# A PSUM bank chosen by its last reader, one more batch transposed by DMA, and key beacons first in the load queue

## The chip, the cores and the metric

The kernel runs on one core of one Trainium2 chip. The metric is the device time of one execution in microseconds (us). Three executions of the kernel before took 357.03, 357.32 and 357.76 us; their median is 357.32 us. A profiled execution, whose trace is read below, took 356.95 us, of which 355.3 us are the span from the first to the last instruction.

## The reference

Attention with 16 "beacon" keys and values ahead of the sequence (8 batches, 8 heads, 576 tokens, head size 64), then a mixer with a low-rank token mix and a two-layer ReLU network.

```python
k_all = np.concatenate([beacon_k, k], axis=2)
v_all = np.concatenate([beacon_v, v], axis=2)
scores = scale * np.matmul(q, k_all.transpose(0, 1, 3, 2))
scores = np.where(causal, -1000000000.0, scores)
a = np.exp(scores - scores.max(-1, keepdims=True))
a /= a.sum(-1, keepdims=True) + 1e-09
attn = np.matmul(a, v_all)                     # -> x: (8, 576, 512)
h = x.transpose(0, 2, 1) @ U @ V               # U: 576x32, V: 32x576
u = x + h.transpose(0, 2, 1)
out = u + np.maximum(u @ w_ch1, 0.0) @ w_ch2   # 512 -> 2048 -> 512
```

## The kernel before

Everything runs in float16 with float32 sums. All instructions of the five engines stand in the order in which the Python program emits them (a manual schedule); engines wait for each other through semaphores only.

**Attention.** Heads go in pairs, four pairs a batch, 32 pairs in all. For a pair the program emits: the transposes of q and k on TensorE into a PSUM tile `tps` (L259, L265), one copy of it to `qT` or `kT` by VectorE (L292, and L297 for the beacons); the scores `sps` (L329), in two visits of four PSUM tiles each (two heads, two groups of key blocks); the exponentials `expt<-sps` on ScalarE (L335); the causal mask on VectorE (L305, L307); and for each head the product with v, `po` (L357, 15 matmuls), which VectorE divides by the sum into `xb` (L365, L366). From batch 4 on, q and k come transposed by DMAs that SyncE issues (`turns`, L607), five for each.

**The token mix of a batch** (`mix_units`) makes `uT`, the transposed u, for that batch. `head` (L393) multiplies the 512 columns of `xb` by U into `qtp` (20 matmuls), VectorE copies it to `qts` (L399). `most` then fills four PSUM tiles `ups`, one for each block of 128 columns, and `end` fills one tile `uend` for the last 80 tokens. It has two forms. Where `turned` is false, TensorE itself adds the transposed x, by 20 matmuls with the identity (`x_into`, L372, 16 in `most` and 4 in `end`); the result is copied out by ScalarE and VectorE in turn (L408, L406). Where `turned` is true, five DMA transposes write x into `uT` first (`turn`, L384), `most` and `end` issue only their four matmuls each with V (L417, L429), and VectorE adds PSUM to `uT` in place (L404, four of 128x496 and one of 128x320). Batch 0 has a form of its own (`first_mix`), batches 1 and 2 are not turned, batches 3 to 7 are. A settled tile of PSUM is free again only when that copy or addition has been done.

**The network** works on nine blocks of 512 tokens. A block has 16 units of the first layer (`gps`, L487, 4 matmuls each, then ReLU at L500 or L502) and 16 of the second (`cps`, L512, four quarters of 4 matmuls to each of four output tiles, then an addition `ob<-cps,ut` at L525 and a store from SyncE at L530). These units lie in a list, `queue`, and are emitted between the units of attention as TensorE's filler. `mix(b)` puts `head`, `most` and `end` of batch b into that list at set distances, `n` units from its front.

**PSUM** has eight banks. All tiles come from one pool with eight buffers and one tag (`pst`); the pool decides which bank a new tile gets. **Loads** are issued by GpSimd. `emit_loads` serves batches 2 and 3 (and the general path that is taken when a sum of exponentials leaves its range, which these inputs don't do): k, then q, then the beacons of k, then the beacons of v and v. VectorE regroups k and q of a pair for the transposes (L252 for tokens, L254 for beacons).

Of the kernel before, what the change touches and what calls it, by code (L numbers as in the profile page):

```python
# [11 lines left out]
F32 = mybir.dt.float32  # L12
# [18 lines left out]
def kernel(  # L31
# [65 lines left out]
    outp = ctx.enter_context(tc.tile_pool(name="outp", bufs=4))  # L97
    small = ctx.enter_context(tc.tile_pool(name="small", bufs=2))
    gen = ctx.enter_context(tc.tile_pool(name="gen", bufs=1))
    psum = ctx.enter_context(tc.tile_pool(name="ps", bufs=8, space=bass.MemoryType.PSUM))  # L100

    def pst(shape, dtype, name):
        return psum.tile(shape, dtype, tag="ps", name=name)


    ident = const.tile([P, P], F16, name="ident", tag="ident")
# [118 lines left out]
        return st, whole  # L225

    def emit_loads(b, L, vs):
        token_load(nc.gpsimd, k[b], L[0][0], ALLH)
        token_load(nc.gpsimd, q[b], L[0][1], ALLH)
        key_beacons(nc.gpsimd, beacon_k[b], L[0][0], ALLH)  # L230
        v_loads(v[b], beacon_v[b], vs)


    def keep_warm(ps, n, a=ident):


        w = ps.shape[-1] // P
        for _ in range(n):
            nc.tensor.matmul(
                ps[:, 0 : w * P].rearrange("p (a b) -> p a b", b=P), a,  # L240
                a.rearrange("p (a b) -> p a b", a=1).broadcast_to([P, w, P]),
                start=True, stop=True,
            )

    def regroup(st, c, i, *copies, beacons=True):

# [35 lines left out]
    def qkT_units(turns, qT, kT, c, copies=((nc.vector.tensor_copy,), (nc.vector.tensor_copy,))):  # L282

        def one(i, dst, b0):
            w = TJ // len(copies[i])
            whole = dst[:, c, b0 : b0 + S].rearrange("x (p j) -> x p j", j=TJ)
            for a, copy in enumerate(copies[i]):
                ps = pst([P, TP * w + b0], F16, name="tps")
                for j in range(w * a, w * a + w):
                    n = TP + b0 if j == TJ - 1 else TP  # L290
                    turns[i](ps, TP * (j - w * a), n, j)
                copy(  # L292
                    out=whole[:, :, ds(w * a, w)],
                    in_=ps[:, 0 : TP * w].rearrange("x (j p) -> x p j", j=w),
                )
            if b0:
                copies[i][0](out=dst[:, c, 0:b0], in_=ps[:, TP * w : TP * w + b0])  # L297

        return [lambda: one(1, qT, 0), lambda: one(0, kT, Nb)]

    def score_units(c, qT, kT, ex, early=False):

        def mask_head(i):
            e4 = ex[i][:, 0:EW].rearrange("p (g w) -> p g w", w=SLOT)[:, :, 0:P]
            nc.vector.tensor_tensor(out=e4, in0=e4, in1=bigmask, op=ALU.min)  # L305
            o, n = blk[(4, 4)], nq[4]
            nc.vector.tensor_tensor(  # L307
                out=ex[i][0:n, ds(o, n)], in0=ex[i][0:n, ds(o, n)], in1=mask[0:n, 0:n], op=ALU.min
            )

        def visit(gs, idle=0, by_head=True, between=None):
            turn = [(g, i) for i in range(2) for g in gs] if by_head else [(g, i) for g in gs for i in range(2)]
            ps = {(g, i): pst([P, 512], F32, name=f"sps{i}") for g, i in turn}
            keep_warm(ps[gs[0], 0], idle)
            if early:
                for g in gs:
                    for i in range(2):
                        for ch, qa, w, o in groups[g]:
                            if ch in (g, 4):
                                n = nq[ch]  # L320
                                nc.tensor.matmul(  # L321
                                    ps[g, i][:, ds(o, n)], identb, negmask[:, min(ch, 1), 0:n],
                                    start=ch == g, stop=False, skip_group_check=True,
                                )
            for g in gs:
                for ch, qa, w, o in groups[g]:
                    for i in range(2):
                        hp = slice(D * i, D * i + D)
                        nc.tensor.matmul(  # L329
                            ps[g, i][:, ds(o, w)], kT[hp, c, ds(P * ch, P)], qT[hp, c, ds(qa, w)],  # L330
                            start=not early, stop=True, skip_group_check=early,
                        )

            def exps(g, i):
                nc.scalar.activation(  # L335
                    out=ex[i][:, ds(SLOT * g, gw[g])], in_=ps[g, i][:, 0 : gw[g]], func=AF.Exp, scale=scale
                )

            for n, (g, i) in enumerate(turn):
                if between and n == len(gs):  # L340
                    between()
                exps(g, i)

        def masks():
            for i in () if early else range(2):
                mask_head(i)

        return [
            lambda idle=0, between=None: visit([0, 1], idle, between=between),
            lambda gs=[2, 3], by_head=True: visit(gs, 0, by_head), masks,  # L350
        ]

    def av_unit(b, h, ex, vs, xb):
        po = pst([P, NT, E], F32, name="po")
        for j in range(NT):
# [10 lines left out]
        nc.vector.tensor_tensor(  # L366
            out=xb[:, :, ds(h * D, D)], in0=po[:, :, 0:D], in1=r.broadcast_to([P, NT, D]), op=ALU.mult
        )

    def x_into(xb, ups, cc, js, a, first):  # L370
        for j in js:
# [5 lines left out]
    def mix_units(xb, u0, turned=True):  # L377
# [10 lines left out]
        def head():  # L388

            qtp = pst([P, P], F32, name="qtp")  # L390
            for j in range(NT):
                for cc in range(NCC):
                    nc.tensor.matmul(  # L393
                        qtp[ds(R * cc, R), :], Usb[: nq[j], j, :], xb[: nq[j], j, ts(cc, P)],
                        start=(j == 0), stop=(j == NT - 1), skip_group_check=True,
                        tile_position=(0, R * cc),
                    )
            qts = small.tile([P, P], F16, name="qts", tag="qts")
            nc.vector.tensor_copy(out=qts, in_=qtp)  # L399
            cell["q"] = qts  # L400

        def settle(i, dst, ups):
# [7 lines left out]
        def most():  # L410
# [8 lines left out]
                )  # L419
            for cc in range(NCC):  # L420
                settle(cc, uT[:, cc, ds(u0, QM)], ups[cc])

        def end():
            n = nq[NT - 1]
# [3 lines left out]
            for cc in range(NCC):  # L428
# [2 lines left out]
                    skip_group_check=True,  # L431
                )
            settle(1, uT[:, :, ds(u0 + QM, n)], ups)

        return turn, head, [most, end]

    def first_mix(xb):
# [4 lines left out]
        def head(c0, n):  # L442
            qtp = pst([R, P * n], F32, name="qtp")
            for j in range(NT):
                nc.tensor.matmul(
                    qtp, Usb[: nq[j], j, :], xb[: nq[j], j, ds(P * c0, P * n)], start=(j == 0), stop=(j == NT - 1)
                )
            nc.vector.tensor_copy(out=qts[0:R, ds(P * c0, P * n)], in_=qtp)

        def begin(c0, n):  # L450
            for cc in range(c0, c0 + n):
# [6 lines left out]
        def rest(c0, n, end):  # L458
# [5 lines left out]
                    )  # L464
            for cc in range(c0, c0 + n):
                act_copy(uT[:, cc, 0:QM], cell[cc])
            end(out=uT[:, ds(c0, n), QM:S], in_=cell["end"])

        return head, begin, rest

    def mlp_units(t0, n, dst, flip, turned=True, last=False):
# [20 lines left out]
        def g_unit(dc):  # L492
# [7 lines left out]
                nc.scalar.activation(out=gT["t"][:, dc, 0:n], in_=g[:, 0:n], func=AF.Relu)  # L500
            else:
                nc.vector.tensor_scalar_max(out=gT["t"][:, dc, 0:n], in0=g[:, 0:n], scalar1=0.0)  # L502

        cps = {}

        def c_unit(i, part):
# [9 lines left out]
            if part == 3:  # L516
# [10 lines left out]
                    nc.scalar.activation(out=ob[:m, :], in_=ps[:m, :], func=AF.Copy)  # L527
                else:
                    nc.vector.tensor_copy(out=ob[:m, :], in_=ps[:m, :])
                nc.sync.dma_start(out=dst(i, m), in_=ob[:m, :])  # L530

        def c_half(i, part):
# [7 lines left out]
            if part % 2:  # L540
                ob = outp.tile([P, DM // 2], F32, name="oh", tag="ob")
                nc.vector.tensor_tensor(out=ob, in0=cps["t"], in1=gT["u"][:, i, hs], op=ALU.add)
                nc.sync.dma_start(out=dst(i, P)[:, hs], in_=ob)

        units += [lambda dc=dc: g_unit(dc) for dc in range(NDC)]
# [22 lines left out]
    def guard_sum():  # L568
        bps = pst([1, 1], F32, name="bps")
        nc.tensor.matmul(bps, bad, ones, start=True, stop=True)  # L570
        nc.vector.tensor_copy(out=badi, in_=bps)


    rows = out.rearrange("b s c -> (b s) c")
# [142 lines left out]

    def mix(b):

        turned = b >= NF and len(queue) >= LAG + 7  # L720
        turn, head, parts = mix_units(xbs[b], S * b, turned)
        if turned:
            turn()
        n = (LAG + 3 * (b == B - 1)) if turned else 2 if b >= NF else 0
        k = 2 if turned else 1
        most, end = parts
        rest = queue[n + k + 3 :]
# [7 lines left out]
    with tc.manual_schedule(engines={ENG.PE, ENG.Activation, ENG.DVE, ENG.SP, ENG.Pool}):  # L735
# [7 lines left out]
                v_beacon(beacon_v[0], vss[0])  # L743
                v_tokens(v[0], vss[0], HALVES[0])
        prs[0][0] = regroup(first, 0, 0, V, act_copy, beacons=False)
        keep_warm(pst([P, 512], F32, name="idle"), IDLE[0], plain)
        t0, sc = qkT_of(0), scores_of(0)
        t0[0]()
        keep_warm(pst([P, 512], F32, name="idle"), IDLE[4])
        t0[1]()  # L750
        sc[0](IDLE[1])
        prs[1] = [None, regroup(first, 1, 1, V)]
# [157 lines left out]
    def safe_head(h, qT, kT, vs, xb):  # L910
        c, hp = h // 2, slice(D * (h % 2), D * (h % 2) + D)
        for j in range(NT):
            n, w = nq[j], min(SK, P * (j + 1))
            sc = utp.tile([P, NC * P], F32, name="sc", tag="ut")
            for o in range(0, w, 512):
# [3 lines left out]
                    sps[:n, 0:m], qT[hp, c, ds(q0[j], n)], kT[hp, c, ds(o, m)], start=True, stop=True  # L919
                )  # L920
                nc.scalar.activation(out=sc[:n, ds(o, m)], in_=sps[:n, 0:m], func=AF.Copy, scale=scale)

            nc.gpsimd.affine_select(
                out=sc[:n, 0:w], in_=sc[:n, 0:w], pattern=[[-1, w]], compare_op=ALU.is_ge, fill=-1.0e9,
# [17 lines left out]
            for cc in range(j + 1):  # L942
# [2 lines left out]
                nc.tensor.transpose(pt[:m, 0:n], pn[:n, ds(P * cc, m)], ident[:n, :n])  # L945
                ptn = gen.tile([P, P], F16, name="ptn", tag="ptn")
                nc.vector.tensor_copy(out=ptn[:m, 0:n], in_=pt[:m, 0:n])
                nc.tensor.matmul(
                    po[:n, :], ptn[:m, 0:n], vs[0:m, ds(cc * H * E + h * E, D)], start=(cc == 0), stop=(cc == j)
                )  # L950
            nc.vector.tensor_copy(out=xb[:n, j, ds(h * D, D)], in_=po[:n, :])

    with tc.If(n_bad != 0, label="general"):
        with tc.For_i(0, B, 1) as bi:
# [48 lines left out]
```

## Time and profile before

| what | value |
|---|---|
| median of three executions | 357.32 us (357.03 to 357.76) |
| the profiled execution | 356.95 us |
| its span | 355.3 us |
| TensorE (PE) busy | 348.2 us of the span, 3130 matmuls |
| VectorE (DVE), ScalarE (ACT) busy | 187.3 us, 167.4 us |
| granted clock of TensorE | 1.00 |
| `L372` ups/uend <- ident,xb | 60 matmuls, 20 of them for batch 2 |
| `L384` uT <- xb (DMA transposes) | 25, from 130.1 us on |

All times within the execution are microseconds from the start of the span. A line of the timeline gives the start, how long the group lasts, the engine, the source line, the operation and its operands, the shape and how many instructions the group holds; in square brackets stands the idle time of the engine just before, and what ended it. Matmuls are pipelined: the duration of one (some 0.38 us for 512 columns) is longer than the distance to the next one (0.216 us), so the costs below are taken from start to start.

### The profile page before, as it was taken

What the parts mean: (1) busy time and instruction counts of PE and PEld (TensorE: products, weight loads), DVE (VectorE), ACT (ScalarE), POOL (GpSimd) and SP (SyncE); (2) the same over time, 40 slices, a digit from 0 to 9 for tenths busy, and PEclk for the clock granted to TensorE, in tenths of its full rate; (3) what the DMA queues carried; (4) which work ended last, traced back from release to release, by engine and by line L of the source; (5) the groups of instructions that cost most, each with busy time, mean ns of one, the idle gap of its engine ahead of it and who ended that gap; (6) DMA issues with size and microseconds to landing.
All of it is one profiled execution on the core that took longest, in us unless ns stands there. A gap on an engine that the chain in (4) does not pass through costs nothing.

```text
span 355.3 us, 7823 instructions
## 1 busy us (share of the span) xinstructions
PE 348.2 (98%) x3130; PEld 174.2 (49%) x3130; DVE 187.3 (53%) x482; ACT 167.4 (47%) x361; POOL 97.5 (27%) x137
## 2 busy tenths in 40 slices
PE   8999999999999999999999999999999999999995
PEld 3665555455554444444444444444454444444443
DVE  5656965588975543754455457345746522313311
ACT  5967841587654563466444664566503202301400
POOL 8956704427437048206800500000000000000000
PEclk9999999999999999999999999999999999999999
DMA  9999999999999979999999993142014413013111
GB/s 181 100 203 169 159 199 171 226 155 123 107 95 149 180 104 131 147 192 104 142 136 178 135 130 81 61 105 52 31 61 102 56 59 105 15 59 100 21 58 67
DMA packets 144170, 41.28 MB, mean 116 GB/s; under 512 B 129024, under 2 KB 139616, under 8 KB 144128
## 3 DMA queue, kind: packets, MB, share of 16 engines
q0 software_dynamic: 87440, 18.18, 66.5%
q1 hardware_dynamic: 56464, 22.25, 33.2%
q8 instruction: 26, 0.43, 0.5%
q10 hardware_dynamic: 224, 0.30, 0.3%
q14 instruction: 16, 0.13, 0.1%
HBM read 37.37 MB, written 9.44 MB: 132 GB/s over the span
## 4 chain that ended last, share of the span: by engine, by line
PE 89%; DMA 3%; DVE 2%; ACT 2%; SPq 1%; issue 0%; ACTq 0%
PE gps L487 34%; PE cps L512 32%; PE po L357 8%; PE sps L329 7%; DMA uT<-xb 2%; ACT expt L335 2%; SPq L384 1%; PE tps L259 1%; DMA stk<-in_k_dram 1%; PE cph L537 1%; PE tps L265 1%; PE ups L372 1%; PE qtp L393 1%; PE sps L321 1%; PE ups L417 1%; DVE uT L404 1%
## 5 line engine op out<-in xcount | busy, mean ns | idle before, releaser
L335 ACT ACTIVATE expt<-sps 128x496 f16<-128x496 f32 (+2 forms) x256 | 111.1, 542 | 57.6 <-PE sps L329 57.5
L487 PE MATMUL gps<-uT,w 128*128 128x512 f16 x576 | 135.7, 379 | 0.1
L512 PE MATMUL cps<-w,gT 128*128 128x512 f16 x560 | 132.7, 380 | 0.0
L500 ACT ACTIVATE gT<-gps 128x512 f16<-128x512 f32 x86 | 51.8, 607 | 94.1 <-PE gps L487 92.3
L487 PEld LDWEIGHTS <-w 128*128 128x128 f16 x576 | 51.9, 98 | 59.5 <-issue 3.8
L512 PEld LDWEIGHTS <-gT 128*128 128x128 f16 x560 | 49.9, 98 | 59.2 <-issue 6.9
L502 DVE TENSOR_SCALAR gT<-gps 128x512 f16<-128x512 f32 x58 | 40.0, 690 | 47.5 <-PE gps L487 46.7
L525 DVE TENSOR_TENSOR ob<-cps,ut 128x512 f32<-128x512 f32 x31 | 21.4, 690 | 49.6 <-PE cps L512 46.7
L207 POOL DMA_DIRECT2D vs<-in_v_dram x50 | 39.6, 809 | 21.4 <-DMA st<-in_k_dram 5.6
L357 PEld LDWEIGHTS <-expt 128*128 128x128 f16 (+1 forms) x960 | 36.2, 98 | 15.1 <-issue 2.6
L357 PE MATMUL po<-vs,expt 128*128 128x65 f16 (+1 forms) x960 | 39.4, 194 | 0.4 <-DVE expt L305 0.3
L329 PE MATMUL sps<-qT,kT 64*128 64x80 f16 (+4 forms) x384 | 34.3, 282 | 0.6 <-DVE uT L404 0.4
L366 DVE TENSOR_TENSOR xb<-po,rec 128x320 f16<-128x320 f32 x64 | 31.5, 492 | 2.2
L305 DVE TENSOR_TENSOR expt<-expt,bigmask 128x512 f16<-128x512 f16 x54 | 22.6, 419 | 11.7 <-ACT expt L335 11.7
L365 DVE RECIPROCAL rec<-po 128x5 f32<-128x5 f32 x64 | 12.0, 187 | 23.9 <-PE po L357 23.9
L329 PEld LDWEIGHTS <-kT 64*128 64x128 f16 x384 | 11.9, 94 | 22.3 <-issue 13.7
L189 POOL DMA_DIRECT2D vs<-in_beacon_v_dram x8 | 4.3, 543 | 61.4 <-PE po L357 61.4
L595 POOL DMA_DIRECT2D st<-in_q_dram x20 | 16.9, 865 | 3.3 <-DMA vs<-in_v_dram 2.2
L595 POOL DMA_DIRECT2D st<-in_k_dram x20 | 16.9, 874 | 0.9 <-DMA vs<-in_v_dram 0.9
L404 DVE TENSOR_TENSOR uT<-ups,uT 128x496 f16<-128x496 f32 x20 | 12.1, 668 | 7.5 <-PE cps L512 3.9
L292 DVE COPY qT<-tps 128x576 f16<-128x576 f16 (+1 forms) x16 | 11.8, 735 | 3.2 <-PE tps L265 2.2
L292 DVE COPY kT<-tps 128x576 f16<-128x576 f16 (+1 forms) x16 | 11.7, 734 | 2.3 <-PE tps L265 1.5
(92 smaller groups left out, 147.2 us busy)
## 6 DMA issues: line engine op xcount, KB each, us to landing
out_dram<-ob SPq DMA_DIRECT2D x35, 256.0 KB, 2.1
vs<-in_v_dram POOLq DMA_DIRECT2D x18, 128.0 KB, 7.7
w<-in_moe_w_ch_dram POOLq DMA_DIRECT2D x4, 512.0 KB, 6.1
w<-in_moe_w_ch_dram POOLq DMA_DIRECT2D x2, 1024.0 KB, 11.6
st<-in_k_dram POOLq DMA_DIRECT2D x12, 128.0 KB, 6.7
st<-in_q_dram POOLq DMA_DIRECT2D x12, 128.0 KB, 9.8
st<-in_k_dram POOLq DMA_DIRECT2D x2, 576.0 KB, 13.1
st<-in_q_dram POOLq DMA_DIRECT2D x2, 576.0 KB, 16.0
```

What stands on the lines that cost most here:

```text
L207: nc.gpsimd.dma_start(out=dst[a : a + nq[j], j, :, :], in_=src[hs, ds(q0[j], nq[j]), :].rearrange("h p d -> p h d"))
L292: copy(out=whole[:, :, ds(w * a, w)], in_=ps[:, 0 : TP * w].rearrange("x (j p) -> x p j", j=w),)
L305: nc.vector.tensor_tensor(out=e4, in0=e4, in1=bigmask, op=ALU.min)
L329: nc.tensor.matmul(ps[g, i][:, ds(o, w)], kT[hp, c, ds(P * ch, P)], qT[hp, c, ds(qa, w)], start=not early, stop=True, skip_group_check=early,)
L335: nc.scalar.activation(out=ex[i][:, ds(SLOT * g, gw[g])], in_=ps[g, i][:, 0 : gw[g]], func=AF.Exp, scale=scale)
L357: nc.tensor.matmul(po[:, j, :], ex[0 : nk[c], ds(blk[(c, j)], P)], vs[0 : nk[c], ds(c * H * E + h * E, E)], start=(c == 0), stop=(c == j),)
L366: nc.vector.tensor_tensor(out=xb[:, :, ds(h * D, D)], in0=po[:, :, 0:D], in1=r.broadcast_to([P, NT, D]), op=ALU.mult)
L487: nc.tensor.matmul(g[:, 0:n], w1[:, cc, ts(dc, P)], uT[:, cc, ds(t0, n)], start=(cc == 0), stop=(cc == NCC - 1))
L500: nc.scalar.activation(out=gT["t"][:, dc, 0:n], in_=g[:, 0:n], func=AF.Relu)
L502: nc.vector.tensor_scalar_max(out=gT["t"][:, dc, 0:n], in0=g[:, 0:n], scalar1=0.0)
L512: nc.tensor.matmul(ps[:m, :], gT["t"][:, dc, ds(P * i, m)], w2[:, dc, :], start=(dc == 0), stop=turned and dc == NDC - 1, skip_group_check ...
L595: nc.gpsimd.dma_start(out=dst[a : m[j], j, :, :], in_=src[:, ds(q0[j], nq[j]), :].rearrange("h p d -> p h d"))
```

## The change

The tile pool of PSUM becomes eight tags with one buffer each. A list `emptied` holds the numbers of the banks that are free, in the order in which their last readers stand in the program; `pst` takes the first, and every place that has emitted the last reader of a tile says so with `emptying`. The filler matmuls that keep TensorE busy at the start get a function of their own, `idle`. In `emit_loads` the beacons of k go ahead of k and q. In `mix` batch 2 becomes turned, with `n` units ahead of its `head`: the lesser of 10 and the length of the list less 8. As built, that list holds 16 units there, so n is 8, where the kernel before had 2 for this batch.

```diff
-    psum = ctx.enter_context(tc.tile_pool(name="ps", bufs=8, space=bass.MemoryType.PSUM))
+    psum = ctx.enter_context(tc.tile_pool(name="ps", bufs=1, space=bass.MemoryType.PSUM))
+
+    emptied = list(range(8))
+    bank_of = {}
 
     def pst(shape, dtype, name):
-        return psum.tile(shape, dtype, tag="ps", name=name)
+
+        b = emptied.pop(0)
+        t = psum.tile(shape, dtype, tag=f"bank{b}", name=name)
+        bank_of[id(t)] = (b, t)
+        return t
+
+    def emptying(t):
+        emptied.append(bank_of.pop(id(t))[0])
...
     def emit_loads(b, L, vs):
+        key_beacons(nc.gpsimd, beacon_k[b], L[0][0], ALLH)
         token_load(nc.gpsimd, k[b], L[0][0], ALLH)
         token_load(nc.gpsimd, q[b], L[0][1], ALLH)
-        key_beacons(nc.gpsimd, beacon_k[b], L[0][0], ALLH)
         v_loads(v[b], beacon_v[b], vs)
...
+    def idle(n, a):
+        ps = pst([P, 512], F32, name="idle")
+        keep_warm(ps, n, a)
+        emptying(ps)
...
             for cc in range(NCC):
                 settle(cc, uT[:, cc, ds(u0, QM)], ups[cc])
+                emptying(ups[cc])
...
     def mix(b):
 
-        turned = b >= NF and len(queue) >= LAG + 7
+        turned = b >= NF
         turn, head, parts = mix_units(xbs[b], S * b, turned)
         if turned:
             turn()
-        n = (LAG + 3 * (b == B - 1)) if turned else 2 if b >= NF else 0
+        n = 0 if not turned else LAG + 3 if b == B - 1 else min(LAG, len(queue) - 8)
```

In `qkT_units` the copy of the beacons (L297) moves into the loop, ahead of the call that frees its tile; the instructions are the same. The same `emptying` call stands behind the last reader of every other PSUM tile (`tps`, `sps`, `po`, `qtp`, `uend`, `gps`, `cps`, and those of the general path).

More of the change, by code (lines that the diff above doesn't have):

```diff
@@ L295, in one @@
                 )
-            if b0:
-                copies[i][0](out=dst[:, c, 0:b0], in_=ps[:, TP * w : TP * w + b0])
+                if b0 and a == len(copies[i]) - 1:
+                    copies[i][0](out=dst[:, c, 0:b0], in_=ps[:, TP * w : TP * w + b0])
+                emptying(ps)
         return [lambda: one(1, qT, 0), lambda: one(0, kT, Nb)]
@@ L342, in visit @@
                 exps(g, i)
+                emptying(ps[g, i])
         def masks():
@@ L368, in av_unit @@
         )
+        emptying(po)
     def x_into(xb, ups, cc, js, a, first):
@@ L399, in head @@
             nc.vector.tensor_copy(out=qts, in_=qtp)
+            emptying(qtp)
             cell["q"] = qts
@@ L433, in end @@
             settle(1, uT[:, :, ds(u0 + QM, n)], ups)
+            emptying(ups)
         return turn, head, [most, end]
@@ L448, in head @@
             nc.vector.tensor_copy(out=qts[0:R, ds(P * c0, P * n)], in_=qtp)
+            emptying(qtp)
         def begin(c0, n):
@@ L466, in rest @@
                 act_copy(uT[:, cc, 0:QM], cell[cc])
+                emptying(cell[cc])
             end(out=uT[:, ds(c0, n), QM:S], in_=cell["end"])
+            emptying(cell["end"])
         return head, begin, rest
@@ L502, in g_unit @@
                 nc.vector.tensor_scalar_max(out=gT["t"][:, dc, 0:n], in0=g[:, 0:n], scalar1=0.0)
+            emptying(g)
         cps = {}
@@ L529, in c_unit @@
                     nc.vector.tensor_copy(out=ob[:m, :], in_=ps[:m, :])
+                emptying(ps)
                 nc.sync.dma_start(out=dst(i, m), in_=ob[:m, :])
@@ L542, in c_half @@
                 nc.vector.tensor_tensor(out=ob, in0=cps["t"], in1=gT["u"][:, i, hs], op=ALU.add)
+                emptying(cps["t"])
                 nc.sync.dma_start(out=dst(i, P)[:, hs], in_=ob)
@@ L571, in guard_sum @@
         nc.vector.tensor_copy(out=badi, in_=bps)
+        emptying(bps)
     rows = out.rearrange("b s c -> (b s) c")
@@ L745 @@
         prs[0][0] = regroup(first, 0, 0, V, act_copy, beacons=False)
-        keep_warm(pst([P, 512], F32, name="idle"), IDLE[0], plain)
+        idle(IDLE[0], plain)
         t0, sc = qkT_of(0), scores_of(0)
         t0[0]()
-        keep_warm(pst([P, 512], F32, name="idle"), IDLE[4])
+        idle(IDLE[4], ident)
         t0[1]()
@@ L921, in safe_head @@
                 nc.scalar.activation(out=sc[:n, ds(o, m)], in_=sps[:n, 0:m], func=AF.Copy, scale=scale)
+                emptying(sps)
             nc.gpsimd.affine_select(
@@ L947, in safe_head @@
                 nc.vector.tensor_copy(out=ptn[:m, 0:n], in_=pt[:m, 0:n])
+                emptying(pt)
                 nc.tensor.matmul(
@@ L951, in safe_head @@
             nc.vector.tensor_copy(out=xb[:n, j, ds(h * D, D)], in_=po[:n, :])
+            emptying(po)
     with tc.If(n_bad != 0, label="general"):
```

## The prediction

> **What bounds the kernel now.** First the page: the engines' busy time, and the chain that ended last.
>
> ```profile
> PE 348.2 (98%) x3130; PEld 174.2 (49%) x3130; DVE 187.3 (53%) x482; ACT 167.4 (47%) x361; POOL 97.5 (27%) x137
> ...
> PE 89%; DMA 3%; DVE 2%; ACT 2%; SPq 1%; issue 0%; ACTq 0%
> ```
>
> TensorE is busy nearly all the time and makes 89% of the chain. A microsecond taken off its stream is a microsecond of time, if no wait takes its place. Next, its waits:
>
> ```profile
> PE idle L239 <- DVE ones L143: 1.2, 1, 1.2
> PE sps L329 <- DVE uT L404: 0.4, 2, 0.2
> PE tps L259 <- DVE pr L252: 0.4, 1, 0.4
> PE po L357 <- DVE expt L305: 0.3, 1, 0.3
> PE sps L321 <- ACT expt L335: 0.2, 1, 0.2
> PE po L357 <- DVE ob L525: 0.2, 1, 0.2
> ```
>
> Little is left to win in waits: two of them (`sps` <- `uT`, `po` <- `ob`) are waits for a PSUM bank in one place, near 183 us. There the matmul pipeline hides part of the loss, so I also look at the starts in the timeline of TensorE:
>
> ```profile
> 182.83 0.38 PE L329 MATMUL sps<-qT,kT 64*128 64x496 f16 x2
> 183.41 0.35 PE L329 MATMUL sps<-qT,kT 64*128 64x464 f16 x1 [0.20 <-DVE uT L404]
> 183.99 0.35 PE L329 MATMUL sps<-qT,kT 64*128 64x464 f16 x1 [0.23 <-DVE uT L404]
> 184.28 1.04 PE L512 MATMUL cps<-w,gT 128*128 128x512 f16 x4
> ```
>
> Four `sps` normally take 0.51 us (103.84 to 104.36); here 1.45. They stand in the banks of four `ups` that VectorE settles one by one from 181.52 to 183.94 us; each is released 0.05 us after its settling. This is the price list for a bank that comes late. Last, the place that the change rewrites, TensorE around the mix of batch 2:
>
> ```profile
> 96.79 0.42 PE L259 MATMUL tps<-ident,pr 96*128 96x96 f16 x6
> 97.14 0.47 PE L393 MATMUL qtp<-xb,Usb 112*32 112x128 f16 x20
> ...
> 98.82 1.05 PE L372 MATMUL ups<-ident,xb 112*128 112x112 f16 x16
> 99.80 0.39 PE L417 MATMUL ups<-Vsb,qts 32*128 32x496 f16 x4
> 100.12 0.44 PE L259 MATMUL tps<-ident,pr 96*128 96x96 f16 x6
> 100.40 1.03 PE L512 MATMUL cps<-w,gT 128*128 128x512 f16 x4
> ...
> 103.46 0.31 PE L372 MATMUL uend<-ident,xb 80*128 80x80 f16 x4
> 103.60 0.31 PE L429 MATMUL uend<-Vend,qts 128*128 128x80 f16 x4
> 103.84 0.58 PE L329 MATMUL sps<-qT,kT 64*128 64x496 f16 x4
> ```
>
> and VectorE's copy after the first of these, SyncE's queue, and what the same transposes take elsewhere:
>
> ```profile
> 97.25 0.76 DVE L292 COPY qT<-tps 128x576 f16<-128x576 f16 x1 [0.15 <-PE tps L259]
> ```
>
> ```profile
> 91.36 1.22 SPq L607 DMA_TRANSPOSE kT<-st  x1
> 102.87 0.35 SPq L530 DMA_DIRECT2D out_dram<-ob  x1
> ```
>
> ```profile
> DMA to landing us min/median/max: 2.4/6.7/9.5
> ```
>
> No matmul stands idle between 96.79 and 104 us: the 20 matmuls at L372 are pure cost. SyncE has nothing to issue between 92.6 (91.36 + 1.22) and 102.87.
>
> **The change, part by part.**
>
> *Removed from TensorE.* 16 matmuls: 99.80 - 98.82 = 0.98 us. Four: 103.60 - 103.46 = 0.14. Together **-1.12 us**. `head`, `most` and `end` keep their other matmuls and only move back. The two copies on ScalarE (L408, 1.06 us together) go too; no matmul waits for them.
>
> *Five transposes on SyncE.* `xb` of batch 2 is complete when the last head's L366 ends at 94.65 us. Five issues 1.26 us apart (L384's median) fill 94.7 to 101.0, inside the idle stretch. What is pushed: the first store still goes near 101; a second store now stands ahead of the second half of batch 4's qT and kT transposes and waits for its `cps`, which ends at 103.5 and is added by 104.3, so that half starts at about 104.8 instead of 103.32. Those landed by 115.8 and are first used by the scores at 120.62; 1.5 us later leaves some 3 us. Cost 0; with that cover gone, each us is one of TensorE. The fourth transpose is issued near 98.6 us and the neighbours in time landed after 4.3 us (issue 91.36) and 3.7 (103.32): 103 us. With the longest landing of the row, 9.5, it is 108.1.
>
> [...]
>
> *The adds on VectorE.* Two casts (1.26 us at 100.25) become four adds in a row (2.42 us, as at 181.52). VectorE is 8.7 of 10 us busy in 93 to 103, and 6.7 in 103 to 113, where the adds now fall.
>
> *The new wait.* I lay the new order out from 97.06 us with the old distances: a quarter of `cps` 0.86 (0.97 ahead of scores), eight `sps` 0.41, four 0.51, `po` 0.46, six `tps` 0.28, `qtp` 0.40. `head` falls near 103.5, the `tps` of the next q near X = 106.6, right behind it the four `ups`, and right behind these eight score matmuls into four tiles. At that point one bank holds `cps`, four hold `ups`. Three remain: the last `sps`, `po`, and this very `tps`. So the second score tile waits for the copy of `tps`, and the fourth for the first `ups`. The copy starts X + 0.46 (96.79 to 97.25), lasts 0.76, and releases after 0.05: X + 1.27. Without a wait TensorE would be there at X + 0.28 + 0.32 = X + 0.60, or X + 0.68 with a change of tile shape as at 96.79 to 97.14. Loss 0.59 to 0.67, say 0.61. The first add follows the copy at X + 0.46 + 0.67, ends at X + 1.80 and releases at X + 1.85; the second pair of score tiles would have come at X + 1.27 + 0.22 = X + 1.49. Loss 0.36. Together **+0.97 us**. No row shows this very wait. From below it is 0 (the copy and the add are done in time); from above 1.55 (the copy's 0.61, and then the 0.94 that the four late adds cost at 182.83). I take 0.97, since each link has its own row.
>
> Queued behind it: VectorE finishes the adds at X + 3.6 = 110.2, then `ob` (cps ends near 110.3) until 111.1, four masks 0.88, the kT copy 0.67 and its beacons 0.15: 112.85. The scores that need this kT come at 113.1. That holds by 0.2 us; what is lost there would add one for one.
>
> *The bank rule.* As built, both programs hand out nearly the same banks: the old pool also gave the bank that had been free longest, so outside batch 2 the matmuls that start within 0.06 us of a release stay the same ones. At 182.83 the four score tiles still take the four `ups` banks, in another order; the last add still ends at 183.94. In the first 17 us some waits move, but ScalarE runs its exponentials there without a gap (31 from 7.49 us on for 13.14, one idle of 0.47), so TensorE only waits elsewhere. Value 0; from below -1.25 (the whole loss at 182.83 to 185.47: 0.94, and 0.31 at `po`), from above +0.1.
>
> *Beacons first.* At 57.7 VectorE waits 1.83 us until 59.56 for batch 2's beacons, though q landed at 59.16. With the beacons ahead, q lands where they did, 59.54, and VectorE goes on 0.2 us earlier. TensorE gains nothing: the scores at 63.49 wait for the kT copy at 62.60, which waited for TensorE's own `tps` (62.13). Batch 3's loads land at 72, ten us before their use. Value 0, from -0.2 to 0.
>
> Sum: -1.12 + 0.97 = **-0.15 us**. The profiled execution goes from 356.95 to 356.8; it stood 0.37 under the median, so on the median's footing 357.32 becomes 357.17, say **357.2 us**.
>
> **The rivals.**
> - *The wait doesn't form.* If VectorE frees `tps` in time, or TensorE reaches the scores later than laid out, the full 1.12 stays: 357.32 - 1.12 = 356.2. For it: every link is only some tenths long. Against: the three banks left are known from the program, and the copy alone (0.76) is longer than the four `ups` (0.32).
> - *The bank rule does more than I grant.* It takes away the losses at 182.83 to 185.47 too: 357.17 - 1.25 = 355.9. Against: four tiles of `ups` and one `cps` leave three banks, whatever the rule.
> - *The transposes land late.* In the batch whose transposes begin at 167.57, the fourth landed at 181.3, 13.8 us after the first issue. From 94.7 that is 108.5, against 107.7 at which the first add could start: the fourth tile and all behind it wait 0.8 us more: 357.17 + 0.8 = 358.0, and 358.4 if the thin 0.2 us at kT breaks and as much again goes there. It decides from a landing at 107.9 on. For it: the row's maximum of 9.5 gives 108.1. Against: near 95 to 103 landings take 3.5 to 4.9 us.
>
> **How the numbers follow.** A measurement of this kernel can tell about 0.2% from no change, 0.71 us. Forecast (net within 0.7): 0.48. No wait: 0.23. Bank rule: 0.09. Late: 0.20, put wholly to slower, with what I have not seen. So faster 0.32, same 0.48, slower 0.20. The likeliest case alone reaches from 356.6 to 357.7. The range holds the no-wait case, half of the bank rule's and the late one's: 355.9 to 358.3.
>
> **What would show it.** After the change: 3110 matmuls; 40 at L372's place instead of 60; 30 transposes `uT<-xb`, the first near 94.7; a start-to-start gap of some 0.6 us at the scores just behind `ups` near 107 us, released by the qT copy, and one of 0.36 released by the first add; the gap near 183 unchanged. I am wrong if those scores start at once, if the adds begin well after the copy (late landing), or if a wait for kT shows near 113.

## The result, and the profile after

The changed kernel takes 355.93 us (median of 8, 355.29 to 356.59) against 357.41 for the kernel before beside it: ratio 0.9960 with a 95% interval of 0.9948 to 0.9973. Timed again later it gave 0.9956 (0.9943 to 0.9970). So it is faster by 0.4%, where 357.2 was forecast and 355.9 to 358.3 was the range. Between the profiled executions the step is the same: 355.51 after 356.95, spans 353.9 and 355.3.

First the page of the changed kernel (busy time, share and count for each engine; then the chain that ended last):

```profile
PE 347.2 (98%) x3110; PEld 173.5 (49%) x3110; DVE 187.8 (53%) x484; ACT 166.2 (47%) x359; POOL 97.6 (28%) x137
...
PE 94%; DMA 2%; DVE 2%; issue 1%; ACT 1%; POOL 0%; POOLq 0%; DVEq 0%
```

The 20 matmuls are gone, and TensorE's share of the chain has grown from 89 to 94%. Its waits, longest first:

```profile
PE idle L249 <- DVE ones L153: 1.2, 1, 1.2
PE tps L280 <- DMA st<-in_k_dram: 0.4, 1, 0.4
PE sps L345 <- DVE qT L307: 0.3, 1, 0.3
PE po L374 <- DVE expt L321: 0.3, 1, 0.3
PE sps L345 <- DVE uT L423: 0.2, 1, 0.2
```

The wait of `po` for `ob` has left the list. Both waits of `sps` are now in the new place, batch 2's mix. The timeline of TensorE there, then that of VectorE, then SyncE's queue with the row of what its five transposes took to land:

```profile
106.74 0.42 PE L274 MATMUL tps<-ident,pr 96*128 96x96 f16 x6
107.09 0.39 PE L436 MATMUL ups<-Vsb,qts 32*128 32x496 f16 x4
107.41 0.31 PE L345 MATMUL sps<-qT,kT 64*128 64x336 f16 x1
108.01 0.37 PE L345 MATMUL sps<-qT,kT 64*128 64x336 f16 x6 [0.28 <-DVE qT L307]
108.59 0.25 PE L345 MATMUL sps<-qT,kT 64*128 64x208 f16 x1 [0.21 <-DVE uT L423]
108.77 2.76 PE L537 MATMUL cps<-w,gT 128*128 128x512 f16 x12
...
113.20 0.58 PE L345 MATMUL sps<-qT,kT 64*128 64x496 f16 x4
...
116.00 0.48 PE L345 MATMUL sps<-qT,kT 64*128 64x336 f16 x8
116.41 1.90 PE L511 MATMUL gps<-uT,w 128*128 128x512 f16 x8
```

```profile
107.20 0.76 DVE L307 COPY qT<-tps 128x576 f16<-128x576 f16 x1 [0.40 <-PE tps L274]
107.87 2.41 DVE L423 TENSOR_TENSOR uT<-ups,uT 128x496 f16<-128x496 f32 x4
...
112.87 0.15 DVE L312 COPY kT<-tps 128x16 f16<-128x16 f16 x1
```

```profile
94.74 6.58 SPq L402 DMA_TRANSPOSE uT<-xb  x5
101.42 3.38 SPq L556 DMA_DIRECT2D out_dram<-ob  x2
104.89 2.29 SPq L635 DMA_TRANSPOSE qT<-st  x1
```

```profile
DMA to landing us min/median/max: 4.3/6.3/7.3
```

The second score matmul starts 0.60 us after the first, released by the copy of `tps`, and the last one waits for the first addition. Without a wait, eight such scores start two by two, the two heads of a pair 0.004 us apart, and take 0.41 us to the next start (116.00 to 116.41); these take 1.36 (107.41 to 108.77) and so lose 0.95. The first wait makes 0.59 of it, since the second score would have started beside the first. The second makes 0.35: from 108.01 on, 0.76 us go by where 0.41 would. The copy of kT ends at 113.02, and its scores start at 113.20 without a wait. The transposes had all landed by 105.3, 2.5 us before the additions began.

The offset between the two traces, taken at the same matmul, is +0.06 us ahead of batch 2's mix and -0.12 from the second `gps` behind it on (116.63 us after the change). So the rewritten place gives 0.18 us. The other 1.26 us come at one place, 182 to 186 us (from -0.12 to -1.38), where I had forecast nothing. TensorE there after the change, then VectorE before and after it:

```profile
182.70 0.58 PE L345 MATMUL sps<-qT,kT 64*128 64x496 f16 x4
183.21 1.04 PE L537 MATMUL cps<-w,gT 128*128 128x512 f16 x4
184.09 0.61 PE L374 MATMUL po<-vs,expt 128*128 128x65 f16 x15
```

```profile
181.52 2.42 DVE L404 TENSOR_TENSOR uT<-ups,uT 128x496 f16<-128x496 f32 x4 [3.89 <-PE cps L512]
```

```profile
179.85 2.42 DVE L423 TENSOR_TENSOR uT<-ups,uT 128x496 f16<-128x496 f32 x4 [2.35 <-DMA uT<-xb]
```

The four `sps` take 0.51 us to the next start; before they took 1.45. By the program they still take banks that `ups` held, but VectorE begins the four additions at 179.85 instead of 181.52. What it waits for is the transposes of batch 4. The row of before names `cps`, which ended at 181.43 but feeds none of these additions; in the trace, VectorE's wait for the semaphore of the fourth transpose lasts until 181.38, and that transpose landed at 181.34. These are the rows of their landing, first before (five issues from 167.6 us), then after (from 167.8):

```profile
DMA to landing us min/median/max: 7.5/8.6/9.5
```

```profile
DMA to landing us min/median/max: 7.1/7.6/7.7
```

The fourth landed at 181.34 before, 179.73 after, although it was issued 0.35 us later after. What held it up shows in the view of the DMA engines, here from 176 to 184 us: 40 slices of 0.2 us, the GB/s that all engines moved in each, and the queue that carries instructions. Before:

```profile
GB/s 158 156 154 150 159 158 141 148 154 159 158 148 161 226 143 140 90 20 13 8 8 10 118 149 114 152 156 163 156 126 147 151 148 156 157 161 156 159 155 153
...
q8 instruction: 1, 0.02, 0.7%
```

After:

```profile
GB/s 160 160 160 157 146 156 146 151 158 159 159 159 157 152 144 159 159 163 159 154 145 139 158 162 157 237 147 148 150 97 6 8 10 9 30 157 157 158 159 159
...
q8 instruction: 1, 0.02, 0.8%
```

One fetch of 16 KB of instructions falls into each window. It is the slice with 226 or 237 (178.6 us before, 181.0 after); its one packet took 0.92 and 1.03 us. Behind it the data queues nearly stop for some 1 us: 8 to 20 GB/s from 179.4 to 180.4 before, 6 to 10 and then 30 from 182.0 to 183.0 after. Before, that hole lies ahead of the fourth landing; after, behind it.

The theory that the experiments test is this: removing 20 matmuls takes 40 instructions out of TensorE's program (PE and PEld both go from 3130 to 3110), so the next fetch of its program, which I took queue q8 to carry, comes that much further on, past the transposes on which the `ups` banks depend. Both pages count 26 such fetches, 0.43 MB, so one comes every 3110 x 2 / 26 = 239 matmuls and weight loads on average. The rivals: the bank rule did it, or the changed order of loads and transposes.

An estimate from these counts: 40/239 of the mean spacing (353.9 / 26 = 13.6 us) is 2.3 us; the fetch moved by 2.4 (178.7 to 181.1).

### The profile page after: what moved, and what is told of

Same layout as the page of the kernel before. It is cut to its first block, busy times and chain, and to the rows that moved or that the text cites. A ratio compares the mean times of both kernels' runs of the same rounds, so it can differ in the third digit from the quotient of the medians.

```text
span 353.9 us, 7832 instructions
## 1 busy us (share of the span) xinstructions
PE 347.2 (98%) x3110; PEld 173.5 (49%) x3110; DVE 187.8 (53%) x484; ACT 166.2 (47%) x359; POOL 97.6 (28%) x137
## 4 chain that ended last, share of the span: by engine, by line
PE 94%; DMA 2%; DVE 2%; issue 1%; ACT 1%; POOL 0%; POOLq 0%; DVEq 0%
PE gps L511 36%; PE cps L537 35%; PE po L374 9%; PE sps L345 8%; DMA st<-in_k_dram 2%; PE tps L274 1%; PE tps L280 1%; PE cph L563 1%; PE qtp L411 1%; PE sps L337 1%; PE ups L436 1%; PE ups L390 0%; DVE kT L307 0%; DVE qT L307 0%; ACT expt L351 0%
## 5 line engine op out<-in xcount | busy, mean ns | idle before, releaser
L374 PEld LDWEIGHTS <-expt 128*128 128x128 f16 (+1 forms) x960 | 36.1, 98 | 14.6 <-issue 2.2
L423 DVE TENSOR_TENSOR uT<-ups,uT 128x496 f16<-128x496 f32 x24 | 14.5, 667 | 6.0 <-PE ups L436 3.6
```

The costliest lines, as they stand in the source:

```text
L374: nc.tensor.matmul(po[:, j, :], ex[0 : nk[c], ds(blk[(c, j)], P)], vs[0 : nk[c], ds(c * H * E + h * E, E)], start=(c == 0), stop=(c == j),)
```

## The experiments

Medians in us, each beside the kernel before in the same series, with the ratio and its interval. "Bank rule", "turned" and "beacons" are the three parts of the change.

| label | kernel | median | before | ratio (95%) |
| --- | --- | --- | --- | --- |
| `bank` | bank rule alone | 356.97 | 357.35 | 0.9995 (0.9983 to 1.0006) |
| `mix` | batch 2 turned, alone | 356.25 | 357.35 | 0.9971 (0.9957 to 0.9985) |
| `beacon` | beacons first, alone | 357.17 | 357.35 | 0.9993 (0.9979 to 1.0008) |
| `bank_mix` | bank rule and turned | 355.88 | 357.35 | 0.9962 (0.9949 to 0.9975) |
| `refill` | changed, 42 instructions added | 356.38 | 356.92 | 0.9979 (0.9966 to 0.9992) |
| `ahead` | before, 128 instructions added | 356.41 | 356.92 | 0.9988 (0.9973 to 1.0003) |
| `n7` | changed, mix one unit later | 355.32 | 356.92 | 0.9951 (0.9936 to 0.9966) |
| `n6` | changed, mix two units later | 355.84 | 356.92 | 0.9966 (0.9953 to 0.9978) |
| `again` | the changed kernel | 355.57 | 357.07 | 0.9956 (0.9943 to 0.9970) |
| `split8` | changed, `ups` in two pairs | 357.71 | 357.07 | 1.0015 (1.0006 to 1.0024) |
| `split8_act` | and two copies on ScalarE | 357.53 | 357.07 | 1.0011 (1.0000 to 1.0023) |
| `n6_act` | n6, two copies on ScalarE | 355.08 | 357.07 | 0.9940 (0.9926 to 0.9954) |

**The parts, one at a time.** Each is the hunk of the change alone, put into the kernel before:

```diff
# bank
-        return psum.tile(shape, dtype, tag="ps", name=name)
+        b = emptied.pop(0)
+        t = psum.tile(shape, dtype, tag=f"bank{b}", name=name)
...
# mix
-        turned = b >= NF and len(queue) >= LAG + 7
+        turned = b >= NF
...
# beacon
+        key_beacons(nc.gpsimd, beacon_k[b], L[0][0], ALLH)
         token_load(nc.gpsimd, k[b], L[0][0], ALLH)
```

> The bank rule alone: batch 2 and the order of the loads are as before. If the rule removes the loss near 183 us (theory 'bank'), the scores there come 0.51 us after one another and the time falls by 1.2 to 1.3 us (0.35%). If the loss went because the fourth transpose of x of batch 4 landed earlier (theory 'landing'), and the rule has no part in that, the loss of 1.25 us stays, the landing is again near 181.3 us, and the time is within 0.2 us of before.

> Batch 2 turned alone, with the old pool of eight buffers and the old order of the loads. Both theories: the region of batch 2 gives 0.15 to 0.2 us, with a wait of some 0.6 us and one of some 0.36 us at the scores behind its ups. Theory 'bank': the loss near 183 us stays, so the time falls by 0.2 us. Theory 'landing', if the shift of the queues by this part moved the landing: the loss near 183 is gone and the time falls by 1.4 us.

> Key beacons first alone. Both theories: VectorE goes on 0.2 us earlier at 59.5 us, TensorE doesn't; the time stays within 0.2 us. Theory 'landing' by the order of the loads: the fourth transpose of batch 4 lands near 179.7 instead of 181.3, the loss near 183 is gone, and the time falls by 1.25 us.

> The whole change without the beacons' part. If the beacons' part is worth nothing: 1.4 us faster than before, like the whole change, with no loss near 183. If the beacons' part moved the landing: 0.2 us faster, with the loss near 183 of 1.25 us back.

Measured: the bank rule alone can't be told from no change, nor can the beacons. Turning batch 2 is worth 1.1 us, though its own place gives only 0.18; neither theory had that, since its profile keeps a loss of 0.79 us near 183 (below). With the bank rule it is worth as much as the whole change. In `bank` the loss near 183 is still there, in two places:

```profile
183.62 0.35 PE L345 MATMUL sps<-qT,kT 64*128 64x464 f16 x1 [0.21 <-DVE uT L423]
183.91 1.04 PE L537 MATMUL cps<-w,gT 128*128 128x512 f16 x4
185.11 0.61 PE L374 MATMUL po<-vs,expt 128*128 128x65 f16 x15 [0.17 <-DVE ob L550]
```

That rules out the bank rule as the cause by itself. In `bank_mix` the loss is gone, and the fetch comes at 181.2 us.

**Putting the fetch back.** The changed kernel with the first eight filler matmuls cut finer. The number of columns is the same, TensorE's program is 42 instructions longer, and all else is as in the change:

```diff
-        idle(IDLE[0], plain)
+        ps = pst([P, 512], F32, name="idle")
+        keep_warm(ps, 1, plain)
+        keep_warm(ps[:, 0:P], 28, plain)
+        emptying(ps)
```

> The whole change, with the first eight idle matmuls of 512 columns written as one of 512 and 28 of 128: the same columns, 42 more instructions in TensorE's program, about as many as the removed matmuls at L372 were. Theory 'fetch': a 16 KB fetch of TensorE's instructions comes at a fixed place of its program; it moves back from 181.1 to some 178.7 us of the span, the fourth transpose of batch 4 lands after 180.7 us instead of 179.7, the gaps at the scores near 183 us are back with 0.6 to 1.25 us between them, and the time is 356.5 to 357.2 us, although batch 2 is turned and the bank rule is in. Rival 'bank order': the loss near 183 us went because of the banks; landing and gaps stay as in the changed kernel, 355.9 us, at most 0.3 more for the start.

From 20 to 180 us its trace is that of the changed kernel within 0.03 us (the start itself differs, by 0.3 us at 12 us). The fetch is back at 177.7 us, the fourth landing at 180.58, and the loss returns; DMA engines, VectorE and TensorE:

```profile
GB/s 161 159 157 147 157 156 148 159 236 148 150 148 131 57 11 8 10 10 111 163 157 154 138 149 159 154 162 150 158 156 152 150 150 149 155 163 153 154 156 154
```

```profile
180.70 2.42 DVE L423 TENSOR_TENSOR uT<-ups,uT 128x496 f16<-128x496 f32 x4 [3.22 <-DMA uT<-xb]
```

```profile
182.68 0.85 PE L345 MATMUL sps<-qT,kT 64*128 64x496 f16 x4
183.45 1.04 PE L537 MATMUL cps<-w,gT 128*128 128x512 f16 x4
184.65 0.61 PE L374 MATMUL po<-vs,expt 128*128 128x65 f16 x15 [0.16 <-DVE ob L550]
```

The hole now lies at 178.8 to 179.6 us. VectorE starts the additions 0.85 us later than in the changed kernel, and TensorE loses 0.59 us. The ratio of the timed runs is 0.9979, where the changed kernel gave 0.9960 and 0.9956: 0.7 to 0.8 us. The intervals of these ratios still overlap a little, so the trace is the stronger evidence. Landing, loss and time each fall a little short of what the theory gave (after 180.7, 0.6 or more, 356.5 or more; measured 180.58, 0.59, 356.38), and well clear of the rival's in the trace. Nothing that computes was touched, so the rival that the banks did it falls.

**Moving it the other way.** The kernel before, unchanged but for fillers that make TensorE's program 128 instructions longer:

```diff
-        keep_warm(pst([P, 512], F32, name="idle"), IDLE[0], plain)
+        ps = pst([P, 512], F32, name="idle")
+        for _ in range(72):
+            nc.tensor.matmul(ps[:, 0:56], plain, plain[:, 0:56], start=True, stop=True)
```

> The kernel before, with the first eight idle matmuls of 512 columns written as 72 of 56: 128 more instructions in TensorE's program, nothing else. Theory 'fetch': the fetch near 178.7 us comes some 7 us earlier, ahead of most of the five transposes' traffic; the fourth lands near 180 us instead of 181.3, the loss of 0.94 + 0.31 us near 183 shrinks by half or more, and the time is 356.3 to 356.9 us, with batch 2 unturned. Rival: the fetch has no part in it; landing and loss stay, 357.4 us, or up to 0.4 more for the start.

```profile
GB/s 158 145 156 154 116 145 157 147 154 155 159 158 161 151 144 154 161 156 153 143 159 157 163 157 159 154 149 152 151 162 148 157 156 161 151 145 147 156 165 233
```

```profile
182.62 0.58 PE L329 MATMUL sps<-qT,kT 64*128 64x496 f16 x4
183.13 1.04 PE L512 MATMUL cps<-w,gT 128*128 128x512 f16 x4
184.01 0.61 PE L357 MATMUL po<-vs,expt 128*128 128x65 f16 x15
```

The fetches fall at 167.8 and 183.9 us (the slice with 233 is the last). The hole behind the first lies at 169.2 to 170.8 us, as the rates from 166 to 174 us show:

```profile
GB/s 149 174 219 254 201 144 113 129 116 194 128 143 145 150 153 144 81 36 28 9 9 10 10 18 134 158 153 156 147 172 156 156 149 97 78 147 142 139 183 142
```

The fourth transpose is issued behind that hole, at 171.83 us, the same time as in the kernel before, and no hole falls while it is in flight. It lands at 179.71 instead of 181.34, so the time of the issue, another rival, doesn't explain the landing. The loss near 183 is gone entirely: 1.26 us at the same matmul, in a kernel with none of the change's parts. The timed median gained 0.5 us, within what was expected, but its interval just includes no change. The profiled execution (355.59 us) was the fastest of twelve (up to 357.49). Where the fetches fell in the others wasn't seen, so the size outside the profile is less sure than the mechanism.

Here are the profiles side by side: TensorE's instructions against the kernel before, start of the fetch, fourth landing, and TensorE's loss near 183 us, as the growth of the offset to the changed kernel between 180 and 200 us at the same matmul.

| label | instructions | fetch | landing | loss |
| --- | --- | --- | --- | --- |
| before | 0 | 178.7 | 181.34 | 1.26 |
| `bank` | 0 | 178.3 | 180.98 | 0.93 |
| `beacon` | 0 | 178.5 | 180.80 | 0.81 |
| `refill` | +2 | 177.7 | 180.58 | 0.59 |
| `mix` | -40 | 180.9 | 180.85 | 0.79 |
| `bank_mix` | -40 | 181.2 | 179.80 | 0 |
| after | -40 | 181.1 | 179.73 | 0 |
| `n7` | -40 | 180.6 | 179.01 | 0 |
| `ahead` | +128 | 167.8, 183.9 | 179.71 | 0 |

Eight rows of nine agree, and so do the traces of `again`, `n6` and `n6_act` (fetch at 180.5, 181.2 and 181.6, landing at 178.75, 178.98 and 180.21, no loss; the last one runs 0.7 us late as a whole). `mix` doesn't: there the fetch came late, and yet the landing was late too. In that trace the data rate fell to 54 and 53 GB/s at 171.6 and 174.8 us, and the second instruction queue had an 8 KB fetch of 1.13 us at 173.2. What made that landing late stays open. Its timed median (356.25) stands nearer to that of `bank_mix` (355.88) than to the kernel before. The loss also varies among kernels with the same count (0.81 to 1.26), so in these eight rows the position of the fetch decides whether there is a loss, and not its exact size. The size follows the landing: from 180.58 to 181.34 us, 0.76 later, the loss grows by 0.67, and `mix` lies on the same line.

**Is the new wait made by the order?** I moved batch 2's mix back by one and by two units of the queue:

```diff
-        n = 0 if not turned else LAG + 3 if b == B - 1 else min(LAG, len(queue) - 8)
+        n = 0 if not turned else LAG + 3 if b == B - 1 else min(LAG, len(queue) - 7)
```

(`n6`: less 6.)

> The whole change, with batch 2's mix placed one queued unit later, so that the four ups stand apart from the transposes whose bank they wait behind, with units of the queue between the ups and the next scores. Theory 'order': the wait of 0.61 + 0.36 us is there only because the scores follow right behind ups with three banks left; it goes, the matmuls behind batch 2's mix stand 0.9 to 1.0 us earlier than in the changed kernel, and the time is about 355.0 us. Rival 'late adds': VectorE or the transposes are late anyway and the wait only moves on (to the scores that follow, or to kT near 113 us): 355.7 to 356.2 us, with a new gap of 0.5 us or more within 20 us behind the mix.

> As the run above, with the mix placed two queued units later. Theory 'order': the same 355.0 us, no gap at the scores. Rival 'late adds': 355.7 to 356.2 us.

The wait at the scores went in both, and another came. In `n7` the fourth `ups` waits, since the eight scores ahead of it hold four banks until ScalarE has read them:

```profile
109.10 0.36 PE L436 MATMUL ups<-Vsb,qts 32*128 32x496 f16 x1 [0.32 <-ACT expt L351]
```

In `n6` the additions stand ahead of the kT copy on VectorE, and the next scores wait for that:

```profile
114.14 0.58 PE L345 MATMUL sps<-qT,kT 64*128 64x496 f16 x4 [0.84 <-DVE kT L312]
```

By the traces `n7` stands 0.27 us ahead of the changed kernel and `n6` 0.16 behind it, where the theory "order" promised 0.9 to 1.0. So the order makes this wait, but a wait moves on, as the rival "late adds" said: `n6` (355.84, a new gap of 0.84) fits it, `n7` (355.32, a gap of 0.32) lies between the two. VectorE is a second limit right behind the banks (0.84 us in `n6`).

**Both limits at once.** `n6_act` leaves `n6` as it is and lets ScalarE, idle from 110.0 to 113.6 us in the changed kernel, copy qT and kT of that head pair:

```diff
         copies = [(act_copy, nc.vector.tensor_copy) if p == 0 else (nc.vector.tensor_copy,)] * 2
+        if p == 15:
+            copies = [(act_copy,)] * 2
```

> The changed kernel itself, timed beside the next three. Every theory: ratio 0.996, 1.3 to 1.5 us under the kernel before; the wait behind ups, some 0.83 us more than full speed, at 107 to 109 us.

> The kernel with the mix two units later (n6), which waited 0.84 us for kT near 114 us, with the same two copies on ScalarE. Theory 'two limits': that wait goes, and the matmuls behind stand 0.7 to 1.0 us earlier than in n6. Rival (the wait is the transposes' or the adds', not the copies'): as n6.

```profile
114.79 0.58 PE L345 MATMUL sps<-qT,kT 64*128 64x496 f16 x4
```

No wait is left there. At equal work the trace stands 0.74 us ahead of the changed kernel, once a start that was 1.47 us late in this execution is taken off, and 0.90 ahead of `n6`. The timed median is 355.08 against 355.57 in the same series: the fastest of all kernels run, though its interval overlaps that of the changed kernel.

**A version that failed.** The four `ups` in two pairs, a unit apart, with and without the copies on ScalarE:

```diff
-        queue[:] = queue[0:n] + [head] + queue[n : n + k] + [most] + queue[n + k : n + k + 3] + [end]
+        if turned and b < B - 1:
+            two = [lambda: most((0, 1)), queue[n + k], lambda: most((2, 3))]
...
+        queue[:] = queue[0:n] + [head] + queue[n : n + k] + two + queue[n + k + 1 : n + k + 3] + [end]
```

> The changed kernel with the four ups of batch 2 made in two pairs, one queued unit apart; same place of the mix. Theory 'two limits' (banks, and right behind them VectorE's queue with 0.2 to 0.3 us to spare at kT): the gaps of 0.46 + 0.37 at the scores go, but the scores near 112.5 us now wait 0.4 to 0.7 for kT's copy; net gain over the changed kernel 0.1 to 0.4 us. Rival 'banks alone': no new wait, 0.8 us under the changed kernel.

> As the run above, and ScalarE copies qT and kT of the head pair whose transposes stand between these units (VectorE did: 0.76, 0.75 and 0.15 us). Theory 'two limits': both waits are gone, the matmuls behind stand 0.7 to 0.9 us earlier than in the changed kernel, the time is 0.6 to 0.9 us under it. Rival 'banks alone': the same as the run above. Rival 'ScalarE in turn': its exponentials come later, a wait at po or at a bank eats more than half of it.

Both lose all that the change had won: `split8` is slower than the kernel before, `split8_act` can't be told from it. In batch 2 it did work: no gap is left at the scores, and at equal work 0.47 and 0.54 us are won. But the condition holds for batches 3 to 6 too, and three of these lose 0.38 to 0.43 us each, the last one 0.7. Part of the reason is in the timeline of `split8`:

```profile
107.56 0.38 PE L436 MATMUL ups<-Vsb,qts 32*128 32x496 f16 x2
...
109.25 0.38 PE L436 MATMUL ups<-Vsb,qts 32*128 32x496 f16 x2
```

Two `ups` take 0.38 us, and so do four (0.39 at 107.09 in the changed kernel). They use 32 rows each and run side by side (in the changed kernel all four start within 0.01 us, 107.09 to 107.10), so cutting the group in two pays that time twice, some 0.31 us from start to start (107.56 to 107.87 in `split8`). Batch 2 pays it too, but its waits go. What else batches 3 to 6 lose stays open. Neither theory had this, and the copies on ScalarE added 0.07 us where 0.4 or more was expected.

## Why the prediction was right and wrong

- *The number fell into the range by luck.* 355.93 lies 0.03 us inside the lower end, 355.9, which the rival cases had set. The likeliest outcome, a net gain too small to tell (0.48), did not come; "faster" had 0.32. Of the gain in the traces, 1.26 us come from a place that the sum put at nothing.
- *The sum for the rewritten place was right.* -1.12 + 0.97 = -0.15 was forecast; -0.18 is measured. The scores behind `ups` wait, released by the two instructions named. The terms are 0.59 and 0.35 us where 0.61 and 0.36 were worked out.
- *The order in time held.* X, the `tps` of the next q, was put at 106.6 and came at 106.74. The kT copy was to end at 112.85 ahead of scores at 113.1, "holds by 0.2"; it ended at 113.02 ahead of 113.20. `n6` shows the price if it breaks: 0.84 us.
- *The transposes on SyncE were hidden, as costed.* They were issued from 94.74 (94.7 forecast). They landed 4.3 to 7.3 us after issue, slower than the 3.7 and 4.3 that I took from the neighbours, but 2.5 us before the additions wanted the last of them. Batch 4's second half went at 104.89 (104.8).
- *Beacons 0 and bank rule 0 were right* within what can be told: 0.9993 and 0.9995.
- *The step that failed is "the gap near 183 unchanged".* I explained that loss by the banks of four `ups`, settled from 181.52 on, and stopped there. The next link was in the same trace: VectorE began at 181.52 because the fourth transpose landed at 181.34, 9.5 us after its issue, the longest of its row. I used the 9.5 as a bound for new transposes, and took the old ones as fixed. They were late behind a 16 KB fetch of instructions at 178.7 us, and with the 20 matmuls removed that fetch came at 181.1. The step was put at 0 and gave 1.26 us.
- *The rival of 355.9 had the place and the size, but not the mechanism.* It let the bank rule take away the loss; alone, the rule leaves it (`bank`), and with the rule in place the loss comes back when the program gets its 42 instructions again (`refill`).

## What to carry to other kernels

Where TensorE waits for a bank, follow the chain past the engine that frees it: if it ends at a DMA that landed later than its neighbours, look at what the DMA engines did in those microseconds before calling the loss fixed. Adding or removing TensorE's instructions moved later fetches here (178.7 to 181.1 us with 40 fewer, 177.7 with 42 put back), so a difference of some tenths of a per cent far from the edit may be the fetch's place and not the edit's merit; a few more, smaller fillers at the start test that without touching the work. And when a wait is designed away, check the next limit in the same place first: here VectorE stood right behind the banks (0.84 us in `n6`), and a group of four matmuls that started within 0.01 us of each other took its 0.31 us a second time when it was cut in two.

## What the runs showed of the hardware

- Behind the 16 KB instruction fetch near 180 us the data transfers had a hole. The packet of that fetch took 0.92 to 1.12 us in the kernel before, the changed one and `refill`, and some 0.7 to 1.1 us after its start the data queues fell from some 155 GB/s to 6 to 20 for about 1 us. In `ahead` the rate was 9 to 36 GB/s from 169.4 to 170.8 us, behind the fetch at 167.8; in `mix`, in slices of 0.4 us, it was 46 and 53 from 182.0 to 182.8, behind the fetch at 180.9. Outside the hole no slice of 0.2 us from 171 to 184 us falls under 45 GB/s before, or under 74 after. In the four profiles whose fetch came at 177.7 to 178.7 us, with the fourth transpose in flight (before, `bank`, `beacon`, `refill`), TensorE lost 0.59 to 1.26 us near 183.
- Not each fetch had such a hole behind it. In the trace before, the one at 48.5 us came beside 205 GB/s, and no slice behind it falls under 179 (46 to 54 us, the fetch in the slice with 276). In `bank`, the fetch at 36.1 us was followed by 8 to 26 GB/s from 36.8 to 37.6 us, without any transpose by DMA in flight. What makes the difference stays open. The row of before:

```profile
GB/s 184 184 195 205 205 205 210 215 200 205 205 205 276 200 189 205 179 220 195 215 215 200 210 200 210 195 207 200 206 191 219 191 204 215 196 204 215 196 204 211
```

- Which engine's program queue q8 carries isn't named in the trace. Its 26 fetches in the kernel before stand beside 6260 matmuls and weight loads, and 482 instructions of VectorE, the next busiest; that, and its moving when only TensorE's instructions were added (181.1 to 177.7 us in `refill`), speak for TensorE. So does a count: the fetch near 180 us comes after 3819 to 3835 of TensorE's matmuls and weight loads in every row of the table but `ahead`, though four of these kernels have 40 fewer of them ahead of the same work. It doesn't come at an exact count: in `ahead` fetches come after 3751 and 4051, and 128 instructions more moved it by 10.9 us, where some 7 were expected.
